# A long convolution and two networks: decodings in three parts, the filter's transform first, and 80 products without a reader

## The chip, the cores and the metric

The kernel runs on one core of a Trainium2 chip. The metric is the device time of one execution in microseconds (us); the kernel before has a median of 1693.93 us over three runs (1693.29 to 1694.32).

## The reference

```python
h_filt = (np.maximum(pos_emb @ w1, 0.0) @ w2) * np.exp(-0.01 * pos)[:, None]
u = x * v
y = irfft(rfft(u, 2 * S, axis=1) * rfft(h_filt, 2 * S, axis=0), axis=1)[:, :S]
t = x * y                                   # S = 12480 tokens, 128 channels
h = t @ moe_w_in                            # 128 -> 2048
g = (a0 + a1*h + a2*h**2 + a3*h**3) / (1 + |b0|*|h| + |b1|*h**2 + 1e-6)
t = g @ moe_w_out                           # 2048 -> 128
h = t @ moe2_w_in
g = where(h >= 1, h, where(h <= -1, 0, (h + 1)**2 / 4))
out = g @ moe2_w_out
```

The four network weights come as 64-bit floats and are decoded to 32 bits on the chip with integer operations.

## The kernel before

**Forward stage** (`conv_transform`, first half). The sequence is laid out as 128 by 49 positions in two halves. Fourteen chunks of 1, 2, eleven times 4, and 2 positions (`CHS`) are loaded: `pt` (positions' embedding), `xt` and `vt`, three DMAs for each chunk from SP (L147 to L149), in three buffers (four for `pt`). For each chunk GpSimd multiplies x by v (`products`, L156), TensorE makes the filter's first layer (`mlp`, L164), ScalarE and VectorE split the result in a high and a low part (`parts`, `split`, L87 and L88), TensorE makes a 128-point transform of each position (six products of 384 columns, L218 to L220), ScalarE and VectorE copy it out (L221, L222), and ACT's queue stores it in `sd` in DRAM (L228).

**Step loop** (second half). The 129 frequencies come in 34 groups: one of 1, thirty-one of 4, two of 2. The loop runs over s, each group passing through it in stages:

- `load` and `load_g` (L248, L121, SP) read a group's `ru` from `sd` and its transform matrices `gg`, five steps ahead.
- `R` (L256) makes the filter's second transform on TensorE, in one PSUM buffer `rp2`; ScalarE and VectorE split it in `rs` (L87, L88).
- `AB` (L267, L268, L270) applies the filter's second layer: four products on the high part of `rs`, two on the low part (L270). ScalarE copies the result to `ab`.
- `U` (L281) makes the signal's second transform, sixteen products, in one PSUM buffer `up`.
- `M` multiplies both: VectorE L298, L299, L301, L302 read `up`, GpSimd L300, L303, L304, L305 add. The result is z.
- `Tr` (L318) transposes z two steps later, and `Inv` (L334) makes the inverse transform three steps later; it goes to `cd` in DRAM, from ACT's queue but for the last three groups (`TQ`), which SP stores (L337).

The order written out in a step is AB(s+1), Tr(s-2, first half), U(s), M(s), R(s+2), Tr(s-2, second half), Inv(s-3). Every engine works through its own instructions in the order written.

**Decodings.** `fillers` makes 32 pieces of work, one for 256 columns of a weight matrix. A piece is a load on SP of 256 KB into `b64` (three buffers), four VectorE operations (L67 to L70), a GpSimd addition (L71), two more VectorE operations (L72, L73) and, for the input weights, a ScalarE copy (L411) and a GpSimd subtraction (L414). `fill(i)` issues everything after the addition of the piece before, then the load of piece i+2, then the first part of piece i. Two are issued before the loop, two in each of the two steps s = -2 and -1, and one in each step from s = 0 to 25.

**Passage to the networks.** After the last group `X0(0)` loads tile 0 of `cd` and of x (L486, L488), `XF` (L496) makes the last inverse transform, `XM` (L501) multiplies by x, `XH` and `XL` (L506, L512) split it, and `h1` begins (L473 to L475). In the three last steps `colsum` makes 16 products of one column for a bias (L432), in PSUM. The networks then run over 196 items of 1024 columns in the order that `ORDER` lists, the second network 11 to 17 items behind the first.

## Time and profile before

| | |
|---|---|
| median of 3 runs | 1693.93 us |
| the profiled execution's own time | 1693.96 us |
| its span, from the first to the last instruction | 1692.2 us |
| busy PE, DVE, ACT, POOL | 1581.5, 1506.0, 1426.9, 1439.9 us |
| mean granted TensorE clock | 0.975 |

Busy time is the time in which an engine has an instruction under way. The granted clock is a share of TensorE's full speed. The span has three parts: the forward stage up to about 105 us, the step loop and its end up to about 385 us, and the networks after that. A stage is read by which engine is busy all through it and by what the others wait for.

### The profile page before, as it was taken

What the parts mean: (1) busy time and instruction counts of PE and PEld (TensorE: products, weight loads), DVE (VectorE), ACT (ScalarE), POOL (GpSimd) and SP (SyncE); (2) the same over time, 40 slices, a digit from 0 to 9 for tenths busy, and PEclk for the clock granted to TensorE, in tenths of its full rate; (3) what the DMA queues carried; (4) which work ended last, traced back from release to release, by engine and by line L of the source; (5) the groups of instructions that cost most, each with busy time, mean ns of one, the idle gap of its engine ahead of it and who ended that gap; (6) DMA issues with size and microseconds to landing.
All of it is one profiled execution on the core that took longest, in us unless ns stands there. A gap on an engine that the chain in (4) does not pass through costs nothing.

```text
span 1692.2 us, 18487 instructions
## 1 busy us (share of the span) xinstructions
PE 1581.5 (93%) x6310; PEld 1063.8 (63%) x6310; DVE 1506.0 (89%) x1524; ACT 1426.9 (84%) x1665; POOL 1439.9 (85%) x883
## 2 busy tenths in 40 slices
PE   6758888986799999999999999999999999999999
PEld 5747777873456656666666666566666666666566
DVE  5549999828999999999999999999999999999990
ACT  4433454546799999999999999999999999999996
POOL 4315676636599999999999999999999999999996
PEclk9877999999899999999999999999999999999999
DMA  9975777631000000000000000000000000000000
GB/s 337 380 259 174 217 216 218 173 100 38 19 13 25 25 1 25 26 26 25 13 13 25 25 26 26 1 25 26 25 25 26 0 26 25 26 16 7 0 7 16
DMA packets 59996, 113.20 MB, mean 67 GB/s; under 512 B 4599, under 2 KB 36607, under 8 KB 58493
## 3 DMA queue, kind: packets, MB, share of 16 engines
q1 hardware_dynamic: 45064, 80.35, 15.4%
q10 hardware_dynamic: 14724, 31.53, 5.1%
q8 instruction: 50, 0.82, 0.2%
q14 instruction: 46, 0.37, 0.1%
q0 software_dynamic: 112, 0.13, 0.0%
HBM read 73.46 MB, written 38.54 MB: 66 GB/s over the span
## 4 chain that ended last, share of the span: by engine, by line
PE 73%; DVE 13%; ACT 6%; DMA 5%; issue 2%; POOL 1%; SPq 0%; ACTq 0%; DVEq 0%; POOLq 0%
PE acc L479 36%; PE h L473 10%; PE h L475 10%; PE h L474 9%; PE acc L496 3%; DMA sd<-so 2%; PE up L281 2%; DVE m L299 1%; DVE m L302 1%; DMA vt<-in_vp_dram 1%; PE cp L334 1%; ACT z L537 1%; DVE t L67 1%; ACT f L533 1%; DVE n L555 1%
## 5 line engine op out<-in xcount | busy, mean ns | idle before, releaser
L546 POOL TENSOR_TENSOR w<-w,z 128x1024 f32<-128x1024 f32 x196 | 470.5, 2400 | 12.3
L632 POOL TENSOR_TENSOR y<-y,c 128x1024 f32<-128x1024 f32 x196 | 468.9, 2393 | 9.8 <-ACT c L628 4.7
L479 PE MATMUL acc<-g,wo 128*128 128x512 f32 (+1 forms) x800 | 373.2, 590 | 12.5 <-DVE g L576 12.5
L479 PE MATMUL acc<-y,wo 128*128 128x512 f32 (+1 forms) x800 | 368.0, 584 | 1.0 <-DVE o L642 0.9
L542 POOL TENSOR_SCALAR w<-z,ab 128x1024 f32<-128x1024 f32 x196 | 235.1, 1199 | 39.9 <-ACT z L537 38.8
L479 PEld LDWEIGHTS acc<-y,wo 128*128 128x128 f32 x800 | 151.6, 190 | 181.4 <-issue 173.0
L576 DVE SCALAR_TENSOR_TENSOR g<-r,n 128x1024 f32<-128x1024 f32 x196 | 240.1, 1225 | 20.7 <-PE h L475 0.5
L555 DVE SCALAR_TENSOR_TENSOR n<-n,co,h 128x1024 f32<-128x1024 f32 x196 | 250.9, 1280 | 6.1
L567 DVE SCALAR_TENSOR_TENSOR n<-n,co,r 128x1024 f32<-128x1024 f32 x196 | 250.2, 1277 | 1.8 <-ACT r L563 1.3
L551 DVE SCALAR_TENSOR_TENSOR n<-f,co,h 128x1024 f32<-128x1024 f32 x196 | 249.5, 1273 | 0.2 <-ACT f L533 0.2
L571 DVE SCALAR_TENSOR_TENSOR r<-w,r 128x1024 f32<-128x1024 f32 x196 | 239.6, 1222 | 0.0
L563 ACT ACTIVATE r<-L 128x1024 f32<-128x1024 f32 x196 | 213.3, 1088 | 20.5 <-DVE g L576 20.5
L479 PEld LDWEIGHTS acc<-g,wo 128*128 128x128 f32 x800 | 149.8, 190 | 123.3 <-issue 93.9
L473 PE MATMUL h<-x1hi,hi 128*128 128x512 f32 (+1 forms) x400 | 214.0, 535 | 13.7 <-DVE n L555 6.8
L559 ACT ACTIVATE L<-w 128x1024 f32<-128x1024 f32 x196 | 216.8, 1106 | 0.0
L615 ACT ACTIVATE y<-h 128x1024 f32<-128x1024 f32 x196 | 210.7, 1075 | 4.6 <-PE h L475 4.5
L537 ACT ACTIVATE z<-h 128x1024 f32<-128x1024 f32 x196 | 208.1, 1062 | 6.0 <-PE h L475 4.6
L533 ACT ACTIVATE f<-h 128x1024 f32<-128x1024 f32 x196 | 208.3, 1063 | 0.0
L473 PE MATMUL h<-x2hi,hi 128*128 128x512 f32 (+1 forms) x400 | 159.3, 398 | 5.9 <-DVE n L555 5.8
L626 ACT ACTIVATE c<-c 128x1024 f32<-128x1024 f32 x147 | 164.7, 1120 | 0.0
L621 ACT ACTIVATE c<-y 128x1024 f32<-128x1024 f32 x147 | 163.8, 1114 | 0.6
L475 PE MATMUL h<-x1lo,hi 128*128 128x512 f32 (+1 forms) x400 | 155.6, 389 | 0.6 <-POOL x1lo L512 0.6
(93 smaller groups left out, 2615.6 us busy)
## 6 DMA issues: line engine op xcount, KB each, us to landing
ru<-sd SPq DMA_DIRECT2D x31, 588.0 KB
sd<-so ACTq DMA_DIRECT2D x11, 1536.0 KB
ct<-cd SPq DMA_DIRECT2D x24, 512.0 KB
cd<-co ACTq DMA_DIRECT2D x30, 392.0 KB
gg<-in_ggc_dram SPq DMA_DIRECT2D x31, 300.1 KB
xTt<-in_xT_dram SPq DMA_DIRECT2D x24, 256.0 KB
out_dram<-o SPq DMA_DIRECT2D x24, 256.0 KB
xt<-in_xp_dram SPq DMA_DIRECT2D x11, 512.0 KB
```

The lines of the kernel that those rows point to most:

```text
L473: nc.tensor.matmul(o, hi[:, f], x[0], start=True, stop=False)
L475: nc.tensor.matmul(o, hi[:, f], x[1], start=False, stop=True)
L479: nc.tensor.matmul(ps, W[l][2][:, f], g[:, k * w:(k + 1) * w], start=f == 0, stop=f == NF - 1)
L533: nc.scalar.activation(s1[i]["f"], s1[i]["h"], AF.Copy, scale=ra3)
L542: nc.gpsimd.tensor_scalar(s["w"], s["z"], ab[:, 1:2], ab[:, 0:1], op0=ALU.mult, op1=ALU.add)
L546: nc.gpsimd.tensor_tensor(s["w"], s["w"], s["z"], op=ALU.mult)
L551: nc.vector.scalar_tensor_tensor(s["n"], s["f"], a[2], s["h"], op0=ALU.add, op1=ALU.mult)
L555: nc.vector.scalar_tensor_tensor(s["n"], s["n"], a[1], s["h"], op0=ALU.add, op1=ALU.mult)
L567: nc.vector.scalar_tensor_tensor(s["n"], s["n"], a[0], s["r"], op0=ALU.add, op1=ALU.mult)
L571: nc.vector.scalar_tensor_tensor(s["r"], s["w"], 1.000001, s["r"], op0=ALU.add, op1=ALU.mult)
L576: nc.vector.scalar_tensor_tensor(s["g"], s["r"], 2.0, s["n"], op0=ALU.subtract, op1=ALU.mult, reverse0=True)
L632: nc.gpsimd.tensor_tensor(s["y"], s["y"], s["c"], op=ALU.add)
```

## The change

The forward stage loads each chunk with one DMA: the host lays x, v and the embeddings side by side (`xvp`), and a chunk has one tile `xt` in three buffers. `products` and `mlp` read that tile. The loads run three chunks ahead rather than four.

A decoding is issued in three parts: the first five operations, in the next `fill` the two after the addition, and in the `fill` after that the ScalarE copy and the GpSimd subtraction. `b64` has seven buffers and loads go ahead by four pieces. Three decodings (`PRE`) stand before the loop, 23 are spread over the steps 1 to 33, and six stand behind the loop (`POST`, four and two). `R(s+2)` moves ahead of the first `Tr` and of `U(s)`.

Tile 0 for the first network goes from `co` straight to a tile `ct0` for the last three groups (one DMA for each frequency, from SP), and from `cd` to `ct0` for the others; its x is loaded at the start of the kernel into `xt0` on the POOL queue. `begin` makes its last transform, product and split inside the convolution's part. `colsum` moves to item 8 of the networks' loop.

Forty products of 384 columns stand behind the last chunk (`sp`), forty of 256 columns behind the last step (`wp`); nothing reads their results.

```diff
 TQ = 3
-CSP = [(0,), (1,), (2, 3)]
+PRE = 3
+POST = 4, 2
+WARM = 40, 40
...
     def load():
-        e["b"] = pool.tile([128, n, 2], I32, name="b64", tag="b64", bufs=3)
+        e["b"] = pool.tile([128, n, 2], I32, name="b64", tag="b64", bufs=7)
-def conv_transform(tc, ident, io, cd, fillers, colsum):
+def conv_transform(tc, ident, io, cd, fillers, xT, begin):
...
         w2l = big.tile([128, NB, D], F32R, name="w2l")
+        ct0 = big.tile([NK, TILES[0] // NB, 2, NB * D], F32, name="ct0")
+        xt0 = big.tile([128, TILES[0] * 128], F32, name="xt0")
+        nc.gpsimd.dma_start(xt0, xT[:, 0:TILES[0] * 128])
...
         fills = fillers(pool("cv_fill", 1))
-        late = []
-        def fill_load(i):
-            if i < len(fills):
-                fills[i][0]()
-        def fill(i):
-            nonlocal late
-            for fn in late:
-                fn()
-            late = []
-            fill_load(i + 2)
-            if i < len(fills):
+        waiting = []
+        loaded = done = 0
+        def fill_load(k):
+            nonlocal loaded
+            for fn in fills[loaded:k]:
+                fn[0]()
+            loaded = max(loaded, min(k, len(fills)))
+        def fill(n=1):
+            nonlocal done
+            for i in range(done, done + n):
+                fill_load(i + 1)
+                later()
...
                     fn()
-                late = fills[i][6:]
+                waiting.append([fills[i][6:8], fills[i][8:]])
+                fill_load(i + 4)
+            done += n
+        def later():
+            for parts in waiting:
+                for fn in parts.pop(0):
+                    fn()
+            waiting[:] = [parts for parts in waiting if parts and parts[0]]
...
                 b = buf[c] = {}
-                b["p"] = ca.tile([128, mx, N1], F32, name="pt", tag="pt", bufs=4)
-                b["x"] = ca.tile([N1, NB, mx, D], F32, name="xt", tag="xt", bufs=XB)
-                b["v"] = ca.tile([N1, NB, mx, D], F32, name="vt", tag="vt", bufs=XB)
-                nc.sync.dma_start(b["p"][:, 0:n], posT[:, m0:m0 + n, :])
-                nc.sync.dma_start(b["x"][:, :, 0:n], xr[:, :, m0:m0 + n, :])
-                nc.sync.dma_start(b["v"][:, :, 0:n], vr[:, :, m0:m0 + n, :])
+                b["a"] = ca.tile([128, mx, 5, 128], F32, name="xt", tag="xt", bufs=XB)
+                nc.sync.dma_start(b["a"][:, 0:n], xvp[:, m0:m0 + n])
...
                 for k in range(NB):
-                    nc.gpsimd.tensor_tensor(st[:, 0:n, k * 256:k * 256 + D], b["x"][:, k, 0:n], b["v"][:, k, 0:n],
+                    nc.gpsimd.tensor_tensor(st[:, 0:n, k * 256:k * 256 + D], b["a"][:, 0:n, k], b["a"][:, 0:n, NB + k],
...
                 for j in range(n):
-                    nc.tensor.matmul(rv[:, j], b["p"][:, j], w1b, start=True, stop=True)
+                    nc.tensor.matmul(rv[:, j], b["a"][:, j, 4], w1b, start=True, stop=True)
...
             loads(2)
-            loads(3)
...
             mlp(0)
+            loads(3)
...
             for c in range(nch):
-                if c + 4 < nch:
-                    loads(c + 4)
+                if 3 < c + 3 < nch:
+                    loads(c + 3)
...
                 nc.scalar.dma_start(sd[:, first[c]:first[c] + n], so[:, 0:n])
-                if c == nch - 4:
-                    for g in range(5):
-                        load_g(g)
-                    fill_load(0)
-                    fill_load(1)
+                if c == nch - 3:
+                    load_g(0)
+                    load_g(1)
+                    fill_load(PRE + 2)
+            sp = cap.tile([128, 2, 512], F32, name="sp", tag="sp", bufs=3)
+            for i in range(WARM[0]):
+                nc.tensor.matmul(sp[:, 0, 0:SIG], f1h[:, 0], b["h"][:, 0], start=True, stop=True)
...
             if h == 0:
-                e["co"] = grp.tile([SL, 4, 256], F32, name="co", tag="co")
+                e["co"] = grp.tile([SL, 4, 256], F32, name="co", tag="co", bufs=3)
...
             if h + 2 == n:
+                if g >= ng - TQ:
+                    for i in range(n):
+                        nc.sync.dma_start(ct0[k0 + i:k0 + i + 1], e["co"][0:TILES[0], i])
+                if g == ng - TQ:
+                    nc.sync.dma_start(ct0[0:k0], cd[0:k0, 0:TILES[0] // NB])
...
             load(g)
-        for i in range(2):
-            fill(i)
-        done = 2
+            if g > 1:
+                load_g(g)
+        fill(PRE)
+        mid = len(fills) - PRE - sum(POST)
...
             on(AB, s + 1)
+            on(R, s + 2)
...
             on(M, s)
-            on(R, s + 2)
...
                 on(Tr, s - 2, 2)
-                if s == ng:
-                    cs = ps.tile([128, 2, 512], F32, name="cs", tag="ap")[:, 0, 0:1]
-                for part in CSP[s - ng]:
-                    colsum(cs, part, 4)
-            for i in range(2 if s < 0 else 1):
-                fill(done)
-                done += 1
+            elif 0 < s and s * mid // (ng - 1) > (s - 1) * mid // (ng - 1):
+                fill()
+            if s == ng - 1:
+                fill_load(len(fills))
+        wp = ps.tile([128, 2, 512], F32, name="up", tag="up")
+        for i in range(WARM[1]):
+            nc.tensor.matmul(wp[:, 0, 0:256], w2h[:, 0], w2h, start=True, stop=True)
+        fill(POST[0])
+        begin(ps.tile([128, 2, 512], F32, name="x0", tag="ap")[:, 0, 0:TILES[0] * 128], ct0, xt0)
+        fill(POST[1])
+        while waiting:
+            later()
...
 @with_exitstack
-def tile_hyena_moe_kernel(ctx, tc, xp, vp, xT, posT, w1, w2, win, sgn, f1c, ggc, fic,
-    def colsum(pt, part, parts):
-        for f in range(part * NF // parts, (part + 1) * NF // parts):
+    def colsum():
+        pt = banks[1][:, 0:1]
+        for f in range(NF):
-        if part == parts - 1:
-            nc.scalar.activation(bias, pt, AF.Copy, scale=-1.0)
+        nc.scalar.activation(bias, pt, AF.Copy, scale=-1.0)
+    x10 = [cp.tile([128, TILES[0] * 128], F32R, name=f"x10{k}") for k in range(2)]
+    def begin(p, ct0, xt0):
+        for j in range(TILES[0]):
+            for r in range(2):
+                nc.tensor.matmul(p[:, j * 128:(j + 1) * 128], ct0[:, j // NB, r, j % NB * D:(j % NB + 1) * D],
+                                 fit[:, r], start=r == 0, stop=r == 1)
+        nc.vector.tensor_tensor(xt0, p, xt0, op=ALU.mult)
+        nc.scalar.copy(x10[0], xt0)
+        nc.gpsimd.tensor_tensor(x10[1], xt0, x10[0].bitcast(F32), op=ALU.subtract)
...
     with tc.manual_schedule():
-        X0(0)
+        x1[0] = x10
-        XF(0)
-        XM(0)
-        XH(0)
-        XL(0)
+            if i == 8:
+                colsum()
...
     x, v, pos = pad(inputs["x"]), pad(inputs["v"]), pad(inputs["pos_emb"])
+    xv = np.stack([x, v]).reshape(2, NB, N1, N2, D).transpose(2, 3, 0, 1, 4).reshape(N1, N2, 2 * NB, D)
+    posT = pos.reshape(NB, N1, N2, 64).transpose(0, 3, 2, 1).reshape(128, N2, 1, N1)
+        "xvp": np.concatenate([xv, posT], 2),
```

## Rows read from the trace of the kernel before

**Rows 1.** Stage, length, busy (instructions) PE, PEld, DVE, ACT, POOL; clock, DMA share, GB/s

```profile
40.00:60.00 20.00, 18.12 (x94) 17.16 (x93) 11.60 (x23) 8.56 (x15) 7.55 (x6) 0.86 1.03 413
120.00:140.00 20.00, 12.35 (x48) 11.60 (x48) 13.96 (x38) 3.81 (x8) 7.45 (x12) 0.50 0.63 185
180.00:200.00 20.00, 18.12 (x127) 15.90 (x126) 19.69 (x32) 9.67 (x18) 13.28 (x15) 1.00 0.78 216
340.00:360.00 20.00, 19.61 (x142) 17.63 (x142) 10.95 (x19) 11.46 (x21) 13.00 (x16) 1.00 0.21 62
```

**Rows 2.** DMA queues from 40 to 60 us: packets, MB, share of 16 engines

```profile
q10 hardware_dynamic: 432, 4.72, 55.8%
q1 hardware_dynamic: 1838, 3.50, 46.4%
```

**Rows 3.** Timeline: start, duration, engine, line, output and input, idle before

```profile
114.79 1.99 PE L256 MATMUL rp<-gg,ru 98*128 98x98 f32 x8
121.99 0.29 DVE L67 TENSOR_SCALAR t<-b 128x256 int32<-128x256 int32 x1 [7.54 <-DMA b<-in_w_in_dram]
124.63 0.41 ACT L411 CAST hi<-w 128x256 fp32r<-128x256 f32 x1 [11.21 <-DVE w L73]
125.70 0.70 PE L267 MATMUL ap<-rs,w2h 128*128 128x392 f32 x1 [8.92 <-ACT rs L87]
130.20 0.28 DVE L67 TENSOR_SCALAR t<-b 128x256 int32<-128x256 int32 x1
```

**Rows 4.** Chain of waits in the forward stage: start, duration, what

```profile
91.03 0.32 PE sp L219
94.78 0.18 PE sp L219
```

**Rows 5.** Timeline: the u products of steps 1, 2, 27, 28 and 31

```profile
134.11 3.57 PE L281 MATMUL up<-gg,ru 98*128 98x98 f32 x16
142.56 2.98 PE L281 MATMUL up<-gg,ru 98*128 98x98 f32 x16
...
325.26 1.93 PE L281 MATMUL up<-gg,ru 98*128 98x98 f32 x16
331.59 1.93 PE L281 MATMUL up<-gg,ru 98*128 98x98 f32 x16
350.15 1.93 PE L281 MATMUL up<-gg,ru 98*128 98x98 f32 x16
```

**Rows 6.** Waits of PE from 145 to 325 us: total, times, longest

```profile
PE ap L270 <- DVE rs L88: 18.9, 25, 1.7
```

**Rows 7.** Timeline: VectorE from one step with a decoding to the next

```profile
284.26 0.56 DVE L298 TENSOR_TENSOR m<-up,ab 128x392 f32<-128x392 f32 x1
287.44 0.80 DVE L72 TENSOR_SCALAR k<-b 128x256 int32<-128x256 int32 x1
291.83 0.56 DVE L298 TENSOR_TENSOR m<-up,ab 128x392 f32<-128x392 f32 x1
```

**Rows 8.** Timeline: VectorE in a step without a decoding

```profile
333.62 0.57 DVE L298 TENSOR_TENSOR m<-up,ab 128x392 f32<-128x392 f32 x1 [3.06 <-PE up L281]
335.46 0.96 DVE L302 TENSOR_TENSOR m<-up,ab 128x784 f32<-128x784 f32 x1
```

**Rows 9.** Timeline: end of the convolution and start of the first network

```profile
361.72 0.56 DVE L302 TENSOR_TENSOR m<-up,ab 128x392 f32<-128x392 f32 x1
365.34 0.95 PE L432 MATMUL cs<-ones,wo 128*128 128x1 f32 x8
377.21 3.48 PE L496 MATMUL acc<-fit,ct 128*128 128x128 f32 x16 [5.93 <-DMA xTt<-in_xT_dram]
380.89 0.69 DVE L501 TENSOR_TENSOR xTt<-acc,xTt 128x512 f32<-128x512 f32 x1 [18.61 <-PE acc L496]
388.25 0.69 DVE L501 TENSOR_TENSOR xTt<-acc,xTt 128x512 f32<-128x512 f32 x1 [6.67 <-PE acc L496]
```

**Rows 10.** Chain of waits there: start, duration, what

```profile
370.29 2.26 DMA cd<-co
```

More of the change, by code (lines that the diff above doesn't have):

```diff
@@ L74, in decode_steps @@
     ]
-def conv_transform(tc, ident, io, cd, fillers, colsum):
+def conv_transform(tc, ident, io, cd, fillers, xT, begin):
     nc = tc.nc
-    xp, vp, posT, w1, w2, win, sgn, f1c, ggc = io
+    xvp, w1, w2, win, sgn, f1c, ggc = io
     with ExitStack() as ctx:
@@ L366, in conv_transform, with kernel @@
                 on(Tr, s - 2, 2)
-                if s == ng:
-                    cs = ps.tile([128, 2, 512], F32, name="cs", tag="ap")[:, 0, 0:1]
-                for part in CSP[s - ng]:
-                    colsum(cs, part, 4)
-            for i in range(2 if s < 0 else 1):
-                fill(done)
-                done += 1
+            elif 0 < s and s * mid // (ng - 1) > (s - 1) * mid // (ng - 1):
[10 more added lines that the diff above has]
+            later()
 @with_exitstack
-def kernel(ctx, tc, xp, vp, xT, posT, w1, w2, win, sgn, f1c, ggc, fic,
+def kernel(ctx, tc, xvp, xT, w1, w2, win, sgn, f1c, ggc, fic,
                           w_in1, w_out1, ca, cb, w_in2, w_out2, out):
@@ L427, in fillers @@
         return parts
-    def colsum(pt, part, parts):
-        for f in range(part * NF // parts, (part + 1) * NF // parts):
+    def colsum():
+        pt = banks[1][:, 0:1]
+        for f in range(NF):
             nc.tensor.matmul(pt, W[1][2][:, f], ones, start=f == 0, stop=f == NF - 1)
-        if part == parts - 1:
-            nc.scalar.activation(bias, pt, AF.Copy, scale=-1.0)
+        nc.scalar.activation(bias, pt, AF.Copy, scale=-1.0)
[8 more added lines that the diff above has]
+        nc.gpsimd.tensor_tensor(x10[1], xt0, x10[0].bitcast(F32), op=ALU.subtract)
     with tc.manual_schedule():
-        conv_transform(tc, ident, (xp, vp, posT, w1, w2, win, sgn, f1c, ggc), cd, fillers, colsum)
+        conv_transform(tc, ident, (xvp, w1, w2, win, sgn, f1c, ggc), cd, fillers, xT, begin)
     nc.scalar.activation(ab, co[:, 4:6], AF.Abs)
@@ L726, in layout @@
     x, v, pos = pad(inputs["x"]), pad(inputs["v"]), pad(inputs["pos_emb"])
+    xv = np.stack([x, v]).reshape(2, NB, N1, N2, D).transpose(2, 3, 0, 1, 4).reshape(N1, N2, 2 * NB, D)
+    posT = pos.reshape(NB, N1, N2, 64).transpose(0, 3, 2, 1).reshape(128, N2, 1, N1)
     a = {
-        "xp": x,
-        "vp": v,
+        "xvp": np.concatenate([xv, posT], 2),
         "xT": x.reshape(NB, N1, N2, D).transpose(3, 2, 0, 1).reshape(D, COLS),
-        "posT": pos.reshape(NB, N1, N2, 64).transpose(0, 3, 2, 1).reshape(128, N2, N1),
         "w1": inputs["w1"],
```

2 lines of the change are left out of this document (removed).

## Prediction

> **What bounds the kernel now.** I read four views in this order: the busy time by stages, the timeline at the two seams of the convolution, the waits of TensorE in the step loop, and the chain of waits. The reader is to see that three stages have three different limits. In the forward stage the DMA engines are full: share 1.03 at 413 GB/s, while TensorE is busy 18.12 of 20 us at a granted clock of 0.86 [rows 1]. In the step loop with decodings VectorE is full, 19.69 of 20 us, and TensorE waits; without decodings TensorE is full, 19.61 of 20 us, and VectorE has time [rows 1]. The networks' part is untouched but for its first items. So the change is worth what it does before 390 us.
>
> All sums are made against the profiled execution's own 1693.96 us, which is 0.03 us from the median; its span is 1692.2 us, and I leave the 1.8 us around it as they are. About 0.2% (3.4 us) is what a measurement of this kernel can tell from no change.
>
> **Forward stage.** The same bytes are loaded: 49 positions of 128 partitions by 5 rows of 512 bytes, 16.06 MB. What changes is the packet, from about 2 KB (3.50 MB in 1838 packets on SP's queue) to 10 KB for a chunk of four. The nearest row for large packets is ACT's queue, 4.72 MB in 432 packets: 55.8% of 20 us, or 2.36 us of all engines for a MB; the loads take 46.4% for 3.50 MB, or 2.65 us [rows 2]. If the new loads cost like those stores, 16.06 x 0.29 = 4.7 us of a full DMA go. I take 4.0, since the stage is not full at its ends. Below, a chunk's tile is free only when GpSimd and the filter's first layer have both read it; eight small products of R take 1.99 us [rows 3], I price that delay with them, and two chunks (2.6 MB, 6.3 us at 413 GB/s) are still under way meanwhile; so it is paid once at most, and the lower end is -2. Fewer load instructions on SP shift nothing else, and the 256 KB for `xt0` on the POOL queue are 0.6 us of DMA time at 413 GB/s, inside that end.
>
> The Trainium skill ("DMA: Bandwidth & Descriptors", Why small descriptors are slow) gives a packet a fixed loss of some 3 cycles beside its 32-byte beats. By that, my estimate from the page is 3.6% of the loads' DMA time, 1.5 us instead of 4.7, and the sum would end 2.5 us later; the rows show the larger difference, and the measured rows decide.
>
> **The first pause.** Now R(1) ends at 116.78, and AB(1) starts at 125.70 after waiting 8.92 us for the split of R(1) on ScalarE [rows 3]. ScalarE stood with the cast of a decoding (L411, idle 11.21 us), which waited for VectorE, which waited 7.54 us for a load of weights [rows 3]. In the new order the decodings before the loop have their five loads issued in the forward stage, and no decoding is issued in steps -2 to 0; their casts come one `fill` later. So AB(1) can follow R(1) by the split, about 0.5 us, as the cast of 256 columns takes 0.41 [rows 3]: 8.4 us gained. The three decodings on VectorE fall between the last chunk and R(0)'s split; at 2.74 us each (three of them from 121.99 to 130.20 [rows 3]) they take 8.2 us and cost nothing while the stores into `sd` and the first `ru` are under way.
>
> The second term is the clock. It is granted at 0.50 from 120 to 140 us, which is the lower of its two levels, 1.2 of 2.4 GHz [rows 1], and sixteen u products take 3.57 and 2.98 us there against 1.93 later [rows 5]. From AB(1) at 125.70 to U(2) at 142.56 two steps take 16.9 us; at 6.33 us (325.26 to 331.59 [rows 5]) they are 12.7, so 4.2 us go if the 40 products hold the clock. They take 0.18 us each at the full level and 0.32 at the lower [rows 4]: 7.2 us, hidden by the pause between the last chunk and R(0), or 12.8 us, which would hold R(0) by some 4 us. I take 8.4 + 4.2 = 12.6. Ends: 4 (lower clock and held, or groups 2 to 4 landing late) and 16.
>
> **The loop.** From U(2) to U(27) there are 25 steps in 182.7 us, 7.31 each [rows 5]; in these TensorE waits 18.9 us, 25 times, for VectorE's half of the split of R before L270 [rows 6]. R moved ahead makes that split a step early, so this wait is gone. What is late next is U: it has one PSUM buffer, and M must have read it. In a step with a decoding VectorE needs 3.18 us for M and the split, and 4.39 for the decoding in the step shown [rows 7], 4.13 on average (7.31 - 3.18). In a step without, M ends at 336.42 [rows 8], U of that step began at 331.59 [rows 5], and the next began 6.33 later at 337.92: 1.5 us to spare. A decoding step overdraws by 7.31 - 6.33 = 0.98 us; a step without one earns it all back. Spread as 23 in 33, seven times two steps with a decoding and three times three stand between steps without. Two overdraw 1.96, which stalls 0.46; three stall 0.46 + 0.98 = 1.44. For 33 steps that is 7.5 us, for the 25 about 5.5. So 25 x 6.33 + 5.5 = 163.8, and 18.9 us are gained, which happens to be the wait of rows 6. Ends: 24.4 without any stall, 7 if every decoding step still takes 7.31 (18 x 7.31 + 7 x 6.33 = 175.9). The steps 27 to 31 have no decoding before and two or three after: -0.5.
>
> The Trainium skill ("GPSIMD Engine Reference", Specifications) says that GpSimd and VectorE share SBUF interfaces and contend when VectorE runs a two-port mode or reads two SBUF inputs. Nothing in the change takes GpSimd's work out of the loop, so by this rule the decodings stay at their dear price there, as the 4.39 beside 2.74 us shows; at the cheap price VectorE would need 5.9 us a step and the 5.5 us of stalls would go.
>
> **The second pause.** Let t be U(31)'s start, 350.15 [rows 5]. Before, M(33) ends at t+12.1 and the last store of `cd` starts at t+20.1 and takes 2.26; the last transform starts at t+27.1 and takes 3.48, and x is multiplied at t+30.7 [rows 9, 10]. After, steps 31 to 33 all have decodings, so M(33) ends near t+16.5 (three of M, of which two are half size, and two of 4.13 behind U(31)), 4.4 us later than now. Some 3 us pass now between z(33) and its transpose, in which TensorE has other steps and the bias products (0.95 us for each eight instructions [rows 9]); so I estimate the last `co` 1.4 us later than now, at t+21.5. SP's issues and a transfer like 2.26 make some 3 us: the last transform can start at t+24.6, 2.5 earlier. The 40 products of 256 columns, 5 us at two thirds of 0.18 each, end about then too. But VectorE has the decoding of step 33 and four more in front of the multiplication: t+16.5 + 5 x 2.74 = t+30.2. So the multiplication comes at t+30.2 instead of t+30.7, and the faster transform is not the end any more. With tile 1's `ct` no longer waiting for its buffer I take +1. The last two decodings are hidden before the multiplication of tile 1 (388.25, VectorE idle 6.67 us before it [rows 9]); if that cover goes, 5 us. Ends: -6 (five decodings at 4.13, x 1.4 more each) and +5 (VectorE not in the way).
>
> **Networks.** The bias products are now 3.8 us of TensorE at item 8, where VectorE is the limit, and ScalarE's bias copy waits for them ahead of item 8's first reading: -0.5, ends 0 and -3.
>
> **Sum.** 4.0 + 12.6 + 18.9 - 0.5 + 1.0 - 0.5 = 35.5; 1693.96 - 35.5 = 1658.5 us.
>
> **Rivals.**
> 1. VectorE still sets every step with a decoding, because `up` has one buffer: 12 us less from the loop, 1670.5. For it: VectorE 19.69 of 20 us. Against: the wait of rows 6 is at L270, and 1.5 us are to spare before U.
> 2. The first pause stays: the clock falls in spite of the products, or they hold R(0) and the groups land late; so the change does not do what it says. 12.6 becomes 4, 1667.1. For it: TensorE waits for DMA between R(0) and R(2), and 0.50 held for long.
> 3. The six decodings behind the loop block the multiplication and the first items: 7 us, 1665.5.
> 4. Slower: the forward stage starves, since one tile for a chunk needs both readers before the next load starts. At worst each of the 11 full chunks shows its transfer (1.31 MB at 413 GB/s, 3.2 us) and 2.26 us of latency, 60 us, and the gain of 4 is lost: 1722. It is slower than before from 3.2 us a chunk on. Against: three buffers as now, share 1.03.
>
> **Chances.** Forecast 0.60 (own range 1650 to 1665), rival 1 0.14, rival 2 0.12, rival 3 0.08, rival 4 0.03, a mixture of losses that cancels to within 0.2% 0.03. Faster 0.94, same 0.03, slower 0.03. The range goes from 1646 (no stalls, upper end at one pause) to 1674 (rival 1 with half of another).
>
> **What would show it.** Right: U to U near 6.4 us with no wait of L270 on the split; granted clock 1.00 from 104 to 145 us; AB(1) before 120 us; SP's loads under 2.5 us a MB; x multiplied behind VectorE's decodings, not behind the transform. Wrong: L281 waiting for M by over 1 us a step; products at 0.32 us; DMA share under 0.9 from 20 to 60 us; networks that start ramping later than their first transform.

## The result and the profile after

The changed kernel takes 1672.59 us (median of four runs, 1669.62 to 1675.15) against 1694.12 us for the kernel before beside it (1693.29 to 1697.74): a ratio of 0.9868 [0.9844, 0.9893], 21.5 us faster. The forecast was 35.5 us, 1658.5. The sign and the range hold; the size is 14 us short of the forecast, and outside its own range of 1650 to 1665.

The profiled execution took 1675.15 us, with a span of 1673.3 and a mean granted clock of 0.981. It is the slowest of the four. Its span is 18.9 us shorter than that of the kernel before, and the 18.9 us are what has to be split up. I took the same marks in both traces; the gain at each is the difference of the two times from the start of the span.

| mark | before | after | gained so far | this stretch | forecast |
|---|---|---|---|---|---|
| last transform product of the forward stage | 103.65 | 99.59 | 4.1 | 4.1 | 4.0 |
| U(2) | 142.56 | 130.74 | 11.8 | 7.8 | 12.6 |
| U(27) | 325.26 | 298.61 | 26.7 | 14.8 | 18.9 |
| U(31) | 350.15 | 325.67 | 24.5 | -2.2 | -0.5 |
| multiplication of tile 0 by x | 380.89 | 357.85 | 23.0 | -1.4 | +1.0 |
| VectorE's first operation of the networks | 388.86 | 369.43 | 19.4 | -3.6 | 0 |
| end of the span | 1692.2 | 1673.3 | 18.9 | -0.5 | -0.5 |

Against the forecast, five stretches came out short: by 4.8, 4.1, 1.7, 2.4 and 3.6 us, 16.6 together. From VectorE's first operation of the networks on, both kernels need the same time, 1303.3 and 1303.9 us. The whole change is decided by when that operation starts.

The stages after answer to [rows 1] (length; busy time and instructions of PE, PEld, DVE, ACT, POOL; granted clock, DMA share, GB/s):

```profile
40.00:60.00 20.00, 17.42 (x95) 15.70 (x94) 11.46 (x23) 9.09 (x16) 7.55 (x6) 0.94 1.00 409
120.00:140.00 20.00, 18.48 (x104) 17.92 (x102) 11.71 (x21) 5.55 (x10) 9.15 (x13) 0.72 0.80 234
180.00:200.00 20.00, 19.22 (x140) 17.73 (x139) 18.08 (x28) 10.96 (x20) 13.81 (x16) 1.00 0.76 222
340.00:360.00 20.00, 14.39 (x93) 11.59 (x90) 15.02 (x40) 6.71 (x13) 9.26 (x14) 1.00 0.56 175
```

DMA is as full in the forward stage as before. In the loop TensorE rose from 18.12 to 19.22 of 20 us and VectorE fell from 19.69 to 18.08. The second row is the surprise: TensorE is busy for 18.48 of 20 us after the pause, but its clock is granted at 0.72 and not at 1.00.

**The first pause.** TensorE's timeline from the last product on (start, duration, engine, line, output and input, idle before) answers to [rows 3]:

```profile
99.59 0.34 PE L230 MATMUL sp<-sl,f1h 128*128 128x384 f32 x1
99.77 7.10 PE L246 MATMUL sp<-sh,f1h 128*128 128x384 f32 x40
109.82 0.43 PE L269 MATMUL rp<-gg,ru 98*128 98x98 f32 x2 [2.95 <-DMA ru<-sd]
...
112.32 2.00 PE L269 MATMUL rp<-gg,ru 98*128 98x98 f32 x8 [0.38 <-DMA ru<-sd]
114.89 0.69 PE L280 MATMUL ap<-rs,w2h 128*128 128x392 f32 x1 [0.57 <-ACT rs L89]
```

AB(1) follows R(1) after 0.57 us instead of 8.92: the split of R no longer stands behind a cast, as forecast. But the clock did not stay. Stretches of 4 us, same columns as above:

```profile
104.00:108.00 4.00, 2.87 (x17) 2.55 (x15) 2.94 (x9) 0.41 (x1) 1.76 (x3) 1.00 0.25 92
108.00:112.00 4.00, 1.79 (x8) 1.49 (x8) 1.20 (x4) 0.27 (x2) 0.72 (x1) 0.85 0.82 248
112.00:116.00 4.00, 3.11 (x11) 2.89 (x12) 0.57 (x1) 0.78 (x2) 0.00 (x0) 0.50 0.96 289
116.00:120.00 4.00, 4.00 (x18) 4.00 (x18) 0.57 (x2) 1.30 (x2) 0.00 (x0) 0.50 0.94 298
...
124.00:128.00 4.00, 4.00 (x18) 4.00 (x18) 1.60 (x3) 0.00 (x0) 0.00 (x0) 0.50 0.80 257
128.00:132.00 4.00, 4.00 (x23) 3.99 (x23) 2.33 (x4) 1.57 (x3) 3.03 (x4) 0.59 0.91 225
```

The forty products end at 106.87 at the full clock. TensorE then waits 2.95 us for the first `ru`, works thinly, and from about 111 to 131 us the clock is granted at 0.50 (1.2 of 2.4 GHz), though TensorE is busy in all of the time from 116 us on. R(1), AB(1) and U(1) run at half speed as before.

**The loop.** Of TensorE's waits between U(2) and U(27), 130 to 299 us (in us, times, longest), these two are all that is left; they answer to [rows 6]:

```profile
PE up L294 <- DVE m L315: 7.9, 11, 0.8
PE ap L283 <- DVE rs L90: 1.3, 1, 1.3
```

**The end.** The timeline from the last step to the first network answers to [rows 9]:

```profile
325.67 3.62 PE L294 MATMUL up<-gg,ru 98*128 98x98 f32 x16 [1.36 <-DVE m L315]
...
347.94 5.14 PE L392 MATMUL up<-w2h 128*128 128x256 f32 x40
353.30 2.02 PE L466 MATMUL x<-fit,ct 128*128 128x128 f32 x16 [0.22 <-DMA cd<-co]
357.85 0.68 DVE L468 TENSOR_TENSOR xt<-x,xt 128x512 f32<-128x512 f32 x1
366.82 0.41 DVE L75 SCALAR_TENSOR_TENSOR wo<-k,t 128x256 f32<-128x256 int32 x1
367.39 1.02 ACT L573 ACTIVATE z<-h 128x1024 f32<-128x1024 f32 x1 [3.32 <-DVE wo L75]
...
369.43 1.28 DVE L587 SCALAR_TENSOR_TENSOR n<-f,co,h 128x1024 f32<-128x1024 f32 x1 [2.20 <-ACT f L569]
```

Three things stand here. U(31) took 3.62 us, at half clock. The transform of tile 0 ends at 355.32, but x is multiplied only at 357.85, behind VectorE's decodings, as forecast. And the first item's reading `z`, whose products had ended at 362.76, waits 3.32 us, by the row for the last decoding's L75.

### The profile page after: what moved, and what is told of

It is laid out like the page before. It is cut to its first block, busy times and chain, and to the rows that moved or that the text cites. A ratio compares the mean times of both kernels' runs of the same rounds, so it can differ in the third digit from the quotient of the medians.

```text
span 1673.3 us, 18627 instructions
## 1 busy us (share of the span) xinstructions
PE 1593.0 (95%) x6390; PEld 1078.7 (64%) x6390; DVE 1504.4 (90%) x1524; ACT 1429.0 (85%) x1665; POOL 1437.9 (86%) x884
## 4 chain that ended last, share of the span: by engine, by line
PE 68%; ACT 5%; DVE 3%; issue 2%; DVEq 0%; ACTq 0%
PE acc L515 36%; PE h L509 10%; PE h L510 10%; PE h L511 10%; PE acc L532 2%; ACT f L569 1%; ACT z L573 1%; DVE n L591 1%; DVE n L587 1%; ACT c L657 1%; ACT L L595 1%; ACT y L651 1%; ACT c L662 1%; DVE n L603 1%; DVE r L607 1%
## 5 line engine op out<-in xcount | busy, mean ns | idle before, releaser
L515 PEld LDWEIGHTS acc<-y,wo 128*128 128x128 f32 x800 | 151.4, 190 | 181.5 <-issue 173.6
L509 PE MATMUL h<-x1hi,hi 128*128 128x512 f32 (+1 forms) x384 | 206.7, 538 | 5.3 <-ACT y L651 4.6
L511 PE MATMUL h<-x2lo,hi 128*128 128x512 f32 (+1 forms) x400 | 154.6, 386 | 0.0
```

The lines of the kernel that those rows point to most:

```text
L509: nc.tensor.matmul(o, hi[:, f], x[0], start=True, stop=False)
L511: nc.tensor.matmul(o, hi[:, f], x[1], start=False, stop=True)
L515: nc.tensor.matmul(ps, W[l][2][:, f], g[:, k * w:(k + 1) * w], start=f == 0, stop=f == NF - 1)
```

## Experiments

Each kernel below is the changed kernel with one edit, timed against the kernel before on the same chip. None of them leaves out any part of the reference. Their marks, in us from the start of the span, with the median and the ratio to the kernel before:

| kernel | first `ru` load | U(2) | U(27) | multiplication by x | first network operation | median | ratio |
|---|---|---|---|---|---|---|---|
| changed kernel, first runs | 106.94 | 130.74 | 298.61 | 357.85 | 369.43 | 1672.59 | 0.9868 [0.9844, 0.9893] |
| changed kernel again | 105.95 | 127.10 | 296.93 | 353.73 | 364.87 | 1671.14 | 0.9855 [0.9840, 0.9871] |
| no products | 106.54 | 125.70 | 293.41 | 351.01 | 362.57 | 1669.81 | 0.9859 [0.9842, 0.9875] |
| second forty only | 104.71 | 124.06 | 291.74 | 349.36 | 360.38 | 1667.94 | 0.9845 [0.9829, 0.9861] |
| first forty only | 106.07 | 127.26 | 297.17 | 354.23 | 365.05 | 1671.71 | 0.9865 [0.9848, 0.9881] |
| first 58 | 110.85 | 129.86 | 297.58 | 355.21 | 366.23 | 1675.12 | 0.9892 [0.9876, 0.9909] |
| five decodings before the loop | 106.16 | 128.48 | 296.21 | 353.00 | 361.31 | 1669.89 | 0.9859 [0.9834, 0.9883] |
| R late again | 108.08 | 132.03 | 308.04 | 370.62 | 381.64 | 1683.78 | 0.9923 [0.9905, 0.9942] |
| decodings in two parts | 106.27 | 129.69 | 297.74 | 354.35 | 364.49 | 1669.12 | 0.9838 [0.9822, 0.9855] |
| three loads a chunk | 110.13 | 131.89 | 301.88 | 358.68 | 369.82 | 1675.00 | 0.9875 [0.9851, 0.9900] |
| products on another operand | 106.13 | 126.67 | 296.44 | 353.21 | 364.28 | 1667.37 | 0.9840 [0.9824, 0.9856] |
| steps 31 to 33 without decoding | 106.59 | 128.00 | 301.57 | 359.31 | 370.34 | 1677.26 | 0.9891 [0.9876, 0.9906] |
| second forty only, five before | 106.62 | 134.53 | 302.38 | 361.63 | 370.59 | 1677.72 | 0.9890 [0.9875, 0.9905] |

In every trace the rest of the span, from the first network operation on, lies between 1303.7 and 1305.3 us, so that column orders the profiled executions (one for each kernel, which need not be the one at its median). The last transform product itself varies by some 2 us between executions (98.6 to 100.7 with one load a chunk), so a start in the first two columns is best read from that product.

### The eighty products

```diff
-WARM = 40, 40
+WARM = 0, 0      (no products)
+WARM = 0, 40     (second forty only)
+WARM = 40, 0     (first forty only)
+WARM = 58, 40    (first 58)
```

**No products** (the other forms of the edit follow, then the changed kernel once more, without an edit)

> The changed kernel without the 80 products. Theory: in the changed kernel the granted clock fell to 0.50 at about 111 us all the same, and the second forty end before VectorE has finished its decodings; so the time stays within 2 us of the changed kernel's 1672.6 us. Rival: the products hold the clock at least for R(0), AB(0) and the last transform, and without them it is 4 us longer (1676.5 us or more). In the trace, U(2) starts within 1 us of 130.7 us by the theory, 2 us or more later by the rival.

**Second forty only**

> Only the second forty products. Theory: as without any before the loop; first pause as in the run without products, and x multiplied at VectorE's pace, 1672.6 us within 2. Rival: the second forty alone spare a cold last transform and first item, 2 us or more below the run without products.

**First forty only**

> Only the first forty products. Theory: the first forty do not hold the clock, since 3 us without work follow them before R(0); 1672.6 us within 2. Rival: they do something for the first steps, and the run is 2 us or more below the run without products.

**First 58**

> Fifty-eight first products instead of forty, so that at 0.175 us each they last from 99.8 to about 110 us, the start of R(0). Theory: the clock was lost in the 3 us between the products and R(0); held, the steps 0 to 2 run at the full level and U(2) starts 4 us earlier, at about 127 us, 1668.5 us in all. Rival: the clock falls anyway in the gaps between R(0) and R(2), where TensorE waits for loads; U(2) stays at 130 us or later and the time does not change, 1672.6 within 2.

**The changed kernel again**

> The changed kernel itself once more, beside the three runs after it: 1672 us, with single executions from 1669 to 1676.

Without any product the kernel is as fast as with all eighty: 0.9859 [0.9842, 0.9875] against 0.9855 [0.9840, 0.9871] for the repeat of the changed kernel and 0.9868 for its first runs. The trace of the kernel without products shows why (stretches of 4 us):

```profile
104.00:108.00 4.00, 0.00 (x0) 0.00 (x0) 2.71 (x9) 0.41 (x1) 1.80 (x3) 0.51 0.51 192
108.00:112.00 4.00, 2.35 (x9) 2.13 (x10) 2.02 (x6) 0.32 (x2) 1.04 (x2) 0.50 0.88 270
112.00:116.00 4.00, 3.42 (x13) 3.18 (x14) 0.57 (x1) 0.73 (x2) 0.00 (x0) 0.50 0.97 286
116.00:120.00 4.00, 3.87 (x22) 3.71 (x22) 1.37 (x5) 1.30 (x2) 0.23 (x1) 0.79 0.93 291
120.00:124.00 4.00, 4.00 (x35) 4.00 (x34) 1.88 (x4) 1.52 (x3) 1.19 (x4) 1.00 0.94 300
```

The clock falls in either case, and comes back in either case. Without products it falls at about 104 us, while TensorE has nothing to do, and is back at about 118, in time for all of U(1). With forty it falls at about 111 and is back at about 131 (108 and 122 in the repeat). The products did not remove the slow stretch, they moved it from the pause onto the work behind it. Fifty-eight hold the clock at 1.00 through the stretch from 108 to 112, but the next stretches read 0.89 and 0.50, so they do not reach R(1) and AB(1) either. In time, from the last transform product to U(2) there are 25.3 us without the first forty (25.4 in the kernel with only the second), 28.5 in the repeat with forty and 29.5 with 58.

In the repeat the clock falls once more inside the loop, at the end of the wait of U(4) for M:

```profile
140.00:144.00 4.00, 4.00 (x20) 3.95 (x20) 3.97 (x6) 0.07 (x1) 3.10 (x5) 0.50 0.07 23
```

It is granted at 0.50 from 139 to 146 us, U(4) takes 3.73 us instead of 2.03, and from U(4) to U(5) there are 10.05 us instead of the 7.77 of the first trace. The same stands in four other traces, all with first products: the first forty only, three loads, another operand and, below, the last steps without a decoding. But for the last, whose loop is another one, U(2) to U(27) takes 169.8 to 170.0 us in these and 167.7 to 168.1 in the rest with R ahead. So from the last transform product to U(27) there are 193.0 and 193.1 us without the first forty, and 198.3, 198.6 and 199.0 with them (the repeat, the first forty only, the first trace).

And they cost something that no row of before could show. From the last transform product to the first load of `ru` there are 6.06 and 6.09 us in the two kernels without the first forty, 7.3 to 7.5 with forty, and 10.53 with 58. The products read `f1h` and the last chunk's `sh`; the suspicion was that `ru` gets the place in SBUF that these tiles leave, so that its load waits for the products' end.

The second forty do what was meant and are worth nothing. In the kernel without them the transform of tile 0 takes 3.57 us instead of 2.02:

```profile
346.55 3.57 PE L466 MATMUL x<-fit,ct 128*128 128x128 f32 x16 [5.07 <-DMA cd<-co]
```

yet from U(33) to the multiplication there are 19.90 us without and 19.93 us with them, since VectorE's decodings end later than either transform. Taken one by one the two halves show no time of their own: the four intervals of 0 and 40 products overlap. In the batch that has both, the eight executions without the first forty take 1669.1 us on average and the four with them, second forty left out, 1671.7: that points the way of the traces, but it was not set up as a comparison of its own. Only 58 are slower than the best of these: 0.9892 [0.9876, 0.9909] against 0.9845 [0.9829, 0.9861].

### Products on another operand

```diff
-WARM = 40, 40
+WARM = 60, 40
...
-            f1h = ca.tile([N1, 2, NK], F32R, name="f1h", bufs=1)
+            f1h = big.tile([N1, 2, NK], F32R, name="f1h")
...
-                nc.tensor.matmul(sp[:, 0, 0:SIG], f1h[:, 0], b["h"][:, 0], start=True, stop=True)
+                nc.tensor.matmul(sp[:, 0, 0:256], f1h[:, 0], f1h, start=True, stop=True)
```

> The first products read only the split transform matrix (kept in a tile of its own to the end of the convolution): sixty of 256 columns, about as long as forty of 384. Theory: in the changed kernel the first load of ru waits until the products have read the forward stage's tiles, whose place it takes (issue at 106.9 us, the products' end; 110.9 with fifty-eight); now it is issued about 6 us after the last transform, as without products, 1.3 us earlier against it, and 1 to 2 us are gained, 1671 us. Rival: that load waits for the stores into sd alone and the products are blameless; its issue stays 7.3 us or more behind the last transform.

Sixty narrower products take as long as the forty, but read only `f1h`, which now lies in a place that `ru` doesn't take. Timeline from the products to R(0), with SP's queue:

```profile
100.26 7.34 PE L246 MATMUL sp<-f1h 128*128 128x256 f32 x60
106.13 1.27 SPq L261 DMA_DIRECT2D ru<-sd  x3
...
108.95 0.43 PE L269 MATMUL rp<-gg,ru 98*128 98x98 f32 x2 [1.36 <-DMA ru<-sd]
```

The load goes out at 106.13, 1.5 us before the products end and 6.05 us after the last transform product (100.08), as in the kernels without products. That shows the cause: it is the operands' place that holds the load, not the products' time on TensorE. The clock is still at 0.50 from 112 to 120 us. The time is 1667.37 us, 0.9840 [0.9824, 0.9856], the lowest median of all; against 0.9855 [0.9840, 0.9871] of the repeat in the same batch the intervals overlap, so that the gain of 1.3 us is shown by the trace and not by the times.

### Decodings before the loop instead of behind it

```diff
-PRE = 3
-POST = 4, 2
+PRE = 5
+POST = 4, 0
```

> Five decodings before the loop and four behind it, so none behind the first multiplication by x. Theory: the first item's reading on ScalarE (z) waited 3.3 us for the last operation of the last decoding and VectorE's first network operation came 11.6 us after the multiplication; both go, 4 to 5 us, and R(0)'s split is held by two decodings before it, about 5 us at U(1): the two nearly cancel, 1672 us within 3. Rival: the split before the loop is not held, since VectorE stands still there, and 4 to 5 us remain as a gain, 1668 us.

The last three marks move as they should: from the multiplication to the first network operation 8.3 us, against 11.1 in the repeat of the changed kernel and 8.0 before the change. `z(0)` now waits for its products instead of a decoding:

```profile
357.97 1.02 ACT L573 ACTIVATE z<-h 128x1024 f32<-128x1024 f32 x1 [3.33 <-PE h L511]
```

So the 3.3 us are the last two decodings', as the changed kernel's row said. But they come back at the other seam: from R(0) to AB(1) it now takes 8.15 us instead of 5.07. The median, 1669.89, is not told apart from the changed kernel's.

I then put together the two edits that looked best, five decodings before the loop and no products there:

```diff
-PRE = 3
-POST = 4, 2
-WARM = 40, 40
+PRE = 5
+POST = 4, 0
+WARM = 0, 40
```

> Only the second forty products, five decodings before the loop and four behind it. Theory: without the first products ru is loaded 1.4 us earlier and the clock comes back 5 us sooner, and the first item no longer waits for the last decodings: 1666 us, 6 us below the changed kernel. Rival: the two gains overlap at the loop's start, where VectorE's five decodings hold R(0)'s split just as long; 1669 us or more.

It is among the slowest, 1677.72 us, 0.9890 against 0.9845 for the second forty only, and its stretches of 4 us say why:

```profile
112.00:116.00 4.00, 1.27 (x6) 1.11 (x6) 2.87 (x8) 0.00 (x0) 1.82 (x3) 0.50 0.96 262
...
132.00:136.00 4.00, 4.00 (x25) 3.99 (x23) 2.12 (x4) 1.57 (x3) 3.24 (x4) 0.62 0.89 233
```

VectorE's five decodings hold the split of R(0); TensorE works 1.27 of 4 us from 112 to 116; the clock, low since about 104, returns only at about 135. U(2) starts 34.0 us after the last transform product, 8.6 us later than with three decodings (25.4), and the clock falls at U(31) too. Two edits that each showed no cost cost 9.8 us together by the medians (1677.72 against 1667.94, in different batches), 7.6 by the ratios; the trace has both of them in the same slow stretch.

### R late again

```diff
             on(AB, s + 1)
-            on(R, s + 2)
...
             on(M, s)
+            on(R, s + 2)
```

> R(s+2) back behind M(s), all else as changed. Theory: VectorE's half of the split stands behind M again, so L283 waits for it in each step with a decoding as before, about 0.76 us a step; the 25 steps from U(2) to U(27) take 8 to 15 us longer, and the time is about 1682 us. Rival: what made the loop faster was only that fewer steps have a decoding (23 in 33 for 26 in 34); then the loop stays within 3 us.

1683.78 us, 0.9923 [0.9905, 0.9942]: 12.6 us slower than the repeat of the changed kernel by the medians, of different batches. TensorE's largest wait between U(2) and U(27) is the old one again:

```profile
PE ap L283 <- DVE rs L90: 11.4, 17, 1.0
```

Seventeen waits, about one for each decoding in these steps. U(2) to U(27) takes 176.0 us: 6.7 less than before the change, from the spread of the decodings (18 instead of 25 in these steps), and 8.1 more than in the changed kernel (167.9). The working's "if every decoding step still takes 7.31" had 175.9. But the clock is in these differences: with R late it stays at 0.50 until 141 us, U(2) takes 3.57 us, and 3.6 of the 8.1 us lie between U(2) and U(3) alone (8.83 us against 5.24). From U(3) to U(27) there are 175.4 us before, 167.2 with R late and 162.6 in the changed kernel: 8.2 us from the spread of the decodings, 4.6 from R's move.

### Decodings in two parts

```diff
-                waiting.append([fills[i][6:8], fills[i][8:]])
+                waiting.append([fills[i][6:]])
```

> Decodings in two parts: the cast on ScalarE and GpSimd's subtraction follow VectorE's last operation in the same place of the order. Theory: ScalarE then waits for VectorE in every other decoding, as before, and holds the copies of the loop behind it; with R's split a step ahead these copies have time, so 3 us at most, 1672 to 1676 us. Rival: the third part is what keeps TensorE going, and without it the steps with a decoding are 0.5 us longer, 10 us in all.

U(2) to U(27) takes 168.05 us, 0.2 more than with three parts, and the time is 1669.12 us, 0.9838 [0.9822, 0.9855]. The wait for which the third part was made appears, but in another place. TensorE's waits between U(2) and U(27), and the wait of ScalarE behind them:

```profile
PE tp L331 <- ACT zt L333: 5.3, 5, 1.3
PE up L294 <- DVE m L315: 4.1, 7, 0.8
```
```profile
ACT hi L435 <- DVE w L75: 18.6, 8, 5.6
```

ScalarE's cast waits for VectorE and so is late with the copy of the transposes, for which TensorE waits 5.3 us; the wait for M shrinks from 7.9 to 4.1. The third part is worth nothing that can be measured here; one wait takes the place of another.

### Three loads a chunk

```diff
-                b["a"] = ca.tile([128, mx, 5, 128], F32, name="xt", tag="xt", bufs=XB)
-                nc.sync.dma_start(b["a"][:, 0:n], xvp[:, m0:m0 + n])
+                b["p"] = ca.tile([128, mx, N1], F32, name="pt", tag="pt", bufs=XB)
+                b["x"] = ca.tile([N1, NB, mx, D], F32, name="xt", tag="xt", bufs=XB)
+                b["v"] = ca.tile([N1, NB, mx, D], F32, name="vt", tag="vt", bufs=XB)
+                nc.sync.dma_start(b["p"][:, 0:n], posT[:, m0:m0 + n, :])
+                nc.sync.dma_start(b["x"][:, :, 0:n], xr[:, :, m0:m0 + n, :])
+                nc.sync.dma_start(b["v"][:, :, 0:n], vr[:, :, m0:m0 + n, :])
...
```

> The forward stage loads each chunk with three DMAs of 2 KB packets again, in the same order and with three buffers each. Theory: the larger packets give 4.2 us of the forward stage, so the last transform ends near 104 us instead of 99.8, and the time is 4 us longer, 1676.5 us. Rival: the forward stage is set by the stores and the waits at its end, and the loads' packets do not matter; the time stays within 1.5 us.

The last transform product comes at 102.65, against 98.6 to 100.7 in all kernels with one load a chunk: 2 to 4 us. The queues from 40 to 60 us (packets, MB, share of 16 engines), first of the changed kernel, where `q1` is SP's loads and `q10` ACT's stores:

```profile
q10 hardware_dynamic: 399, 4.31, 51.9%
q1 hardware_dynamic: 423, 3.85, 48.3%
```

then the loads of the kernel with three:

```profile
q1 hardware_dynamic: 2022, 3.86, 51.0%
```

Packets of 9.1 KB take 48.3% of 20 us for 3.85 MB, 2.51 us of all engines a MB; those of 1.9 KB take 2.64, as before the change (2.65 [rows 2]). Over the longer stretch from 20 to 70 us it is 2.49 to 2.57 in all twelve traces with one load a chunk, and 2.66 and 2.67 with three and before the change. The time, 1675.00 us, 0.9875 [0.9851, 0.9900], does not tell the two kernels apart; the traces do.

### The last steps without a decoding

```diff
-            elif 0 < s and s * mid // (ng - 1) > (s - 1) * mid // (ng - 1):
+            elif 0 < s <= ng - 4 and s * mid // (ng - 4) > (s - 1) * mid // (ng - 4):
```

> The 23 decodings of the loop stand in steps 1 to 30, none in the three last ones. Theory: U(31) to U(33) took 12.25 us in the changed kernel, against 9.4 before, because VectorE comes late to M and the clock falls there; without decodings it is 9.4 to 9.9 and the second multiplication is 3 us earlier against U(31), while denser decodings cost 1.3 us more in the loop: 1670.5 us. Rival: VectorE's backlog is only moved to the decodings behind the loop, and nothing is gained, 1672.5 us or more.

1677.26 us, 0.9891 [0.9876, 0.9906], slower than the repeat in the same batch by 6.1 us. Twenty-three decodings in thirty steps make the loop longer: 173.6 us from U(2) to U(27), 3.7 more than the repeat's 169.8, both with the second slow stretch in them. And the end gave nothing back: U(31) to U(33) takes 10.61 us against 10.53. The timeline of U(31) and U(32) shows what is late:

```profile
329.13 2.03 PE L294 MATMUL up<-gg,ru 98*128 98x98 f32 x16 [1.36 <-DVE m L315]
336.16 1.13 PE L294 MATMUL up<-gg,ru 98*128 98x98 f32 x8 [1.75 <-DVE m L315]
```

Both wait for the M of the step before. The theory that decodings in the steps 31 to 33 stretch the end fell: a row of steps that each have one, before the end, leaves VectorE behind just as far.

## Why the prediction was right and wrong

The mechanisms were mostly the ones described, and so were the sign of the whole and the order of its three large terms. Two steps of the working failed, "4.2 us go if the 40 products hold the clock" and "The last two decodings are hidden before the multiplication of tile 1", and one term, the loop's 18.9, was too large.

**Forward stage, 4.0 forecast: right in size.** 4.1 us at the last product, 3.0 at the first `ru` load. The loads fell from 2.65 to 2.51 us a MB, not to the stores' 2.36, so that the queues explain 16.06 x 0.14 = 2.2 us of it; the rest lies within the 2 us by which that product varies, so that the hit is partly luck; and the sign asked for, loads under 2.5 us a MB, was just missed. The Trainium skill ("DMA: Bandwidth & Descriptors", Why small descriptors are slow) came to 1.5 us by my estimate, a little below the measured 2.2, where my row for stores came to 4.7: the page's fixed loss a packet was nearer than the row I preferred. Rival 4, a stage that starves, did not occur: the DMA share from 20 to 60 us is 1.01.

**The first pause, 12.6 forecast: 7.8.** The first half was right: the wait of AB(1) went from 8.92 to 0.57 us, 8.4 us less, as forecast. The second half failed. From AB(1) to U(2) there are 15.8 us instead of 16.9, so that 1.0 of the 4.2 us came. In the repeat there are 13.3, and 3.5 us came; but there the second slow stretch takes 2 us back in the loop, which no term of the working had. Rival 2's ground, the clock falling in spite of the products, is what happened, and the kernel without products says that they were not even of use. The step had taken it that products which hold the clock until R(0) hold it through U(2). But TensorE stands again behind them, for the first `ru`, and the clock fell there, right ahead of the work it was meant for. Another 1.1 us went to `ru`, held by the products' operands, and 0.4 to the wait from its issue to R(0); 4.1 + 8.2 + 1.0 - 1.1 - 0.4 = 11.8, which is the gain at U(2), with 8.2 for the stretch from R(0) to AB(1).

**The loop, 18.9 forecast: 14.8.** Right: the wait at the split went, the next to be late is U, behind M in the one buffer of `up`, and it stalls only after two steps with a decoding in a row. The size was off by the stall. (In the repeat, with the slow stretch at U(4), the gain is 12.9.) VectorE's timeline in two steps with a decoding, the start of the decoding and of the split behind it, and one operation within:

```profile
230.77 0.28 DVE L74 TENSOR_SCALAR k<-b 128x256 int32<-128x256 int32 x1
...
232.08 0.98 DVE L69 TENSOR_SCALAR t<-b 128x256 int32<-128x256 int32 x1
...
234.81 0.56 DVE L90 TENSOR_TENSOR rs<-rp,rs 128x392 fp32r<-128x392 f32 x1
...
242.99 0.28 DVE L74 TENSOR_SCALAR k<-b 128x256 int32<-128x256 int32 x1
...
247.57 0.56 DVE L90 TENSOR_TENSOR rs<-rp,rs 128x392 fp32r<-128x392 f32 x1
```

The decodings take 4.04 and 4.58 us, 4.31 on average, where the working had 4.13. A step with one overdraws by 4.31 + 3.18 - 6.33 = 1.16 us instead of 0.98, two by 2.32, and 1.5 are earned back: a stall of 0.82 instead of 0.46. Measured are 11 waits of 0.72 on average. With 7.9 + 1.3 us of waits, 25 steps of 6.33 make 167.5 us, and 167.9 are there. So this term is settled: 9.2 us of stalls where 5.5 were expected, and a fifth of a us in the price of a decoding made the larger part of that. The working took 4.13 from the old order. With R late again the decodings take 3.87 and 4.39 us, 4.13 on average, as before the change: it is the new order, with the decoding right behind M and the split behind both, that made them dearer, and the working had not priced that. Rival 1, a full VectorE in every step with a decoding, fell: the wait is 0.8 us at most, in 11 of 25 steps.

The rows also bear out why a decoding is dear. L69 takes 0.98 us here beside GpSimd's part of M, and 0.29 behind the loop, where GpSimd does nothing at that moment:

```profile
234.02 0.41 DVE L71 SCALAR_TENSOR_TENSOR t<-b,t 128x256 int32<-128x256 int32 x1
...
246.14 0.78 POOL L438 TENSOR_TENSOR lo<-w,hi 128x256 fp32r<-128x256 f32 x1
246.25 0.95 DVE L71 SCALAR_TENSOR_TENSOR t<-b,t 128x256 int32<-128x256 int32 x1
...
346.73 0.29 DVE L69 TENSOR_SCALAR t<-b 128x256 int32<-128x256 int32 x1
```

L71, which reads two operands in SBUF, takes 0.95 us beside GpSimd's subtraction and 0.41 just after GpSimd's last part of M. The Trainium skill's rule on shared SBUF interfaces ("GPSIMD Engine Reference", Specifications) names VectorE's instructions in a two-port mode and those with two SBUF inputs; the trace agrees for L71. L69 has one input, and which mode it runs in no trace here shows.

**Steps 27 to 31, -0.5 forecast: -2.2.** 27.06 us instead of 24.89, in this execution and in the repeat alike. The decodings that now stand there cost as in the loop; the forecast had priced two or three of them at 0.2 us each.

**The second pause, +1.0 forecast: -1.4 in this execution.** From U(31) to the multiplication there are 32.18 us, where the working said 30.2. In the repeat it is 29.74, and 29.72 or 29.73 with five decodings before the loop, with two parts, with three loads and on another operand: 30.74 - 29.73 = 1.0, as forecast, and set by VectorE's decodings, as forecast. What the profiled execution has besides is the clock: granted at 0.50 from 326 to about 333 us, in U(31) and the work behind it.

```profile
326.00:328.00 2.00, 2.00 (x11) 2.00 (x11) 0.00 (x0) 0.00 (x0) 1.92 (x3) 0.50 0.04 8
```

U(31) took 3.62 us there and 2.03 in the repeat. The same came in the executions with R late (3.57) and with five decodings and only the second forty (3.64); without products, with the second forty only and with 58 the clock fell just behind U(31), and the stretch to the multiplication was 30.5 us; in the others it did not fall. It makes 2.4 us here, and so a part of the spread from 1669.6 to 1675.2 us. TensorE waits 1.36 us for M ahead of U(31) in both kinds of execution, so that wait alone does not decide it.

**The first items, hidden by the forecast: -3.6.** The working hid the last two decodings under VectorE's 6.67 us of idle time before tile 1's multiplication [rows 9], and gave 5 us as the price if that cover goes. It did not hold, as VectorE's timeline shows:

```profile
364.75 0.29 DVE L74 TENSOR_SCALAR k<-b 128x256 int32<-128x256 int32 x1
366.21 0.69 DVE L537 TENSOR_TENSOR xTt<-acc,xTt 128x512 f32<-128x512 f32 x1 [1.17 <-PE acc L532]
```

Tile 1's multiplication (L537) stands ahead of the last operation of the last decoding (L75 at 366.82), and itself waits 1.17 us for TensorE's transform. `z(0)` waits for that L75, 3.32 us. The clock has a part in it: it is granted at 0.50 from 360 to 366 us, tile 1's transform takes 3.62 us there against 2.02 for tile 0's, and the 1.17 us that L537 waits for it hold L75, and so `z`, about as long. `z` does not read the weights that L75 writes, only `h` in PSUM; what is left by the code is the place in SBUF of `z`, which the decodings' tiles had before. This is argued from the code and was not tried by itself; that the two decodings make the wait is shown by the kernel that has them before the loop. What should have been read was not when VectorE is idle, but who waits for the last decoding. Rival 3 had this, at 7 us and a chance of 0.08; half of it came.

**The networks, -0.5 forecast: -0.5.** 1303.3 and 1303.9 us; since the executions of this part, unchanged in all the experiments, spread over 1.6 us, this is no test of the term.

Range and chances: 1672.59 lies near the upper end of the range, where the forecast's losses add up, and close to rival 1's 1670.5 by time but not by mechanism. What I gave too little weight is that the terms erred to one side: five came out short, by 1.7 to 4.8 us, and only the forward stage and the networks by nothing. Of the signs named ahead, the granted clock of 1.00 from 104 to 145 us is the one that failed outright: it was 0.50 from 111 to 131.

Open: what makes the clock fall near steps 4 and 31 in some executions; what sets the length of a slow stretch behind the first pause, some 14 us in one trace of the changed kernel and 20 in the other; and what the first forty products cost: from the last transform product to the first network operation their traces have 266 us and more against 262 without them, the pooled executions 2.6 us, and the intervals of the single kernels overlap.

## What to carry to other kernels

Products that were only to hold the clock were worth nothing here: a thin stretch lay between them and the dense work, and they moved a slow stretch onto useful work. Whether products that reach the dense work would do better, no run here shows. Before such instructions are added, look at what their operands' place in SBUF is needed for: a product without a reader still holds its operands, and the load behind them. When work is spread evenly over an engine's spare time, sum its price at the end of the longest run of loaded steps, with the price taken from the stretch where it will stand: errors of 0.2 us in one piece come back many times over.

## What the runs showed of the hardware

In the changed kernel's trace TensorE was busy in all of 15 us, from 116 to 131, at a granted clock of 0.50, and only then did it rise; in the kernel without products, with the same work in the same order, it was back at about 118 us, behind a stretch in which TensorE was busy 3.42 of 4 us (112 to 116). I had expected dense work to bring it back at the same pace each time. And in one and the same kernel the clock fell near step 31 in one execution and near step 4 in the other, though both have the same waits there (1.36 us for U(31), 0.78 and 0.77 us for U(4)).
